# Reordering the first eight loads of a fused attention and gated-MLP kernel: the first Q weights between token tiles 0 and 1, K weights ahead of tile 2

## The chip, the cores and the metric

The kernel runs on one core of a Trainium2 chip. The metric is the device time of one execution in microseconds (us), taken over several executions. A profile gives one of these executions instruction by instruction. Its span is about 1.75 us shorter than the device time of the same execution (268.9 against 270.63 us).

In every text below, tile 0, 1, 2 … are the blocks of 128 tokens of the input, and "Q rows 0-2" are the first three of five 128-row blocks of the Q part of the weight matrix. In profile lines PE is TensorE and PEld its weight loads, DVE is VectorE, ACT is ScalarE, POOL is GpSimd and SP is SyncE; L640 is line 640 of the kernel. XST holds the token tiles as loaded, XNS normalised, XNT also transposed; PS is PSUM, the memory that PE writes its results to.

## The reference, cut to what matters

```python
xn = _layernorm(x)                       # 2048 tokens x 640
qkv = xn @ wqkv                          # 640 -> 3 x 640: Q, K, V
# 32 heads of 20, each token attends to itself and 7 earlier ones, two apart; softmax; weighted V; @ wo
g, u = xn @ w_gate, xn @ w_up            # 640 -> 1536 each
return x + attention(...) @ wo + (g * u) @ w_down
```

Only the head matters here: a token tile is loaded, normalised, transposed, and multiplied by Q, K and V weights.

## The kernel before

The Python program holds a small list scheduler. Each piece of work is a task with a priority, and the scheduler, using its own model of durations and landings, fixes at build time the order of instructions on each engine. So a change in the order of loads changes the *modelled* landings, and through them the order of instructions on all engines.

The loads at the head, all issued by SyncE on one queue:

```python
def x_load(t, eng="sp"):                       # one token tile, 160 KB
    dma(XST[:, xslot(t), :], xhbm[t * TS:(t + 1) * TS, :], ...)

def wqkv_load(g, lo=0, hi=NCH):                # g: 0 Q, 1 K, 2 V; rows lo..hi of five, 160 KB each
    dst = WQKV[:, WPOS[g], lo:hi, :]
    dma(dst, wqkv_src[:, lo:hi, g * D:(g + 1) * D], ...)
# ... cut ...
x_load(0)
# a small touch load on ACT's queue
x_load(1)
wqkv_load(0, 0, 3)
wqkv_load(0, 3, NCH)
x_load(2)
wqkv_load(1, 0, 3)
wqkv_load(1, 3, NCH)
x_load(3)
K.t["act"] = 2.1
warm(18)                                       # 18 filler matmuls on zeros
```

What happens to a tile (cut to the engines and their order):

```python
def front(t):
    # DVE: bn_stats of two halves (L538), bn_aggr (L541); ACT: sqrt (L544); DVE: reciprocal (L549)
    # DVE: apply -> XNS (L556); PE: five transposes into PSUM (L585); tile 0: three filler matmuls (L624)
    # copy out of PSUM -> XNT: tile 0 DVE three blocks (L595) and ACT two (L597); others DVE (L604)
    for i in range(2):
        # ... cut ...
        yield Task("dve", lambda: stats(i), r=[x], prio=-1 if t == 1 and i == 0 else p)
```

The first half of tile 1's statistics has the priority -1: once tile 0's square root is scheduled, it goes ahead of all that is left of tile 0 on DVE. Then PE multiplies (L640): for tile 0, twenty 128-column matmuls with Q, twenty with K; the same for tile 1; ten 256-column matmuls for both tiles together; then tiles 2, 3 and so on, and after them V with 512 columns.

## Time and profile before

| | |
|---|---|
| time, median of 3 (lowest to highest) | 270.04 us (269.69 to 270.15) |
| span of the profiled execution | 268.9 us |
| PE busy | 262.7 us, 98% |
| first projection matmul starts | 7.30 us |
| loss between tile 1's transposes and its first matmul | 0.75 us |

Two lines of the page of the kernel before: busy time of the engines, and the chain of waits that ended last, by engine.

```profile
PE 262.7 (98%) x1765; PEld 152.8 (57%) x1783; DVE 222.9 (83%) x282; ACT 105.4 (39%) x188; POOL 130.3 (48%) x81
...
PE 94%; DMA 2%; DVE 2%; issue 1%; SPq 0%; DVEq 0%
```

PE is busy 98% of the span and makes 94% of the chain. What can be won or lost is therefore the time before PE's unbroken run begins. The timeline of the kernel before, at its head; the columns are start, duration, engine, line, operation, output and inputs, form, count, and in brackets the idle time of that engine just before and what ended it.

```profile
3.22 0.89 DVE L538 BATCH_NORM_STATS2 STATS<-XST 128x6 f32<-128x320 bf16 x2 [1.98 <-DMA XST<-in_A_x_dram]
...
5.42 0.71 PE L585 MATMUL PS<-IDENT,XNS 128*128 128x128 bf16 x5
...
5.96 0.36 DVE L595 COPY XNT<-PS 128x384 bf16<-128x384 bf16 x1 [0.20 <-PE PS L585]
...
7.30 1.48 PE L640 MATMUL PS<-XNT,WQKV 128*128 128x128 bf16 x20 [0.53 <-DMA WQKV<-in_A_wqkv_dram]
...
8.61 0.44 PE L585 MATMUL PS<-IDENT,XNS 128*128 128x128 bf16 x5
...
9.09 0.49 DVE L604 COPY XNT<-PS 128x640 bf16<-128x640 bf16 x1
...
9.64 1.98 PE L640 MATMUL PS<-XNT,WQKV 128*128 128x128 bf16 x32 [0.59 <-DVE XNT L604]
```

Read PE's lines. Its first projection matmul at 7.30 waits for weights although tile 0's copy ended at 6.32 (5.96 + 0.36). Tile 1's transposes come at 8.61; their copy on DVE runs from 9.09 to 9.58, and PE sits idle 0.59 us until it restarts at 9.64. The last transpose began at 8.84 and would have freed PE 0.06 us later, so 0.75 us are lost from start to start. From 9.64 the matmuls follow each other without a gap. The chain of waits of the same kernel in its first 30 us (start, length, what) says the same:

```profile
1.73 5.44 DMA WQKV<-in_A_wqkv_dram
...
9.09 0.50 DVE XNT L604
```

The first line is the load of Q rows 0-2: issued at 1.73, landed at 7.17.

### The profile page before, as it was taken

What the parts mean: (1) busy time and instruction counts of PE and PEld (TensorE: products, weight loads), DVE (VectorE), ACT (ScalarE), POOL (GpSimd) and SP (SyncE); (2) the same over time, 40 slices, a digit from 0 to 9 for tenths busy, and PEclk for the clock granted to TensorE, in tenths of its full rate; (3) what the DMA queues carried; (4) which work ended last, traced back from release to release, by engine and by line L of the source; (5) the groups of instructions that cost most, each with busy time, mean ns of one, the idle gap of its engine ahead of it and who ended that gap; (6) DMA issues with size and microseconds to landing.
All of it is one profiled execution on the core that took longest, in us unless ns stands there. A gap on an engine that the chain in (4) does not pass through costs nothing.

```text
span 268.9 us, 4464 instructions
## 1 busy us (share of the span) xinstructions
PE 262.7 (98%) x1765; PEld 152.8 (57%) x1783; DVE 222.9 (83%) x282; ACT 105.4 (39%) x188; POOL 130.3 (48%) x81
## 2 busy tenths in 40 slices
PE   7899999999999999999999999999999999999996
PEld 5796975444444444444444445765457654676775
DVE  4678899999999997379999899999999989992212
ACT  3369998556723232245344353024430342201000
POOL 1000000000004439900199999999999879985000
PEclk9999999999999999999999999999999999999999
DMA  6954479621414998087025953465534561022201
GB/s 206 367 188 74 98 105 339 247 97 56 142 39 113 234 244 177 0 268 151 2 52 140 240 118 79 132 176 138 152 79 130 148 195 42 27 73 61 87 28 49
DMA packets 40261, 35.58 MB, mean 132 GB/s; under 512 B 15408, under 2 KB 38448, under 8 KB 40240
## 3 DMA queue, kind: packets, MB, share of 16 engines
q1 hardware_dynamic: 39424, 33.15, 45.4%
q0 software_dynamic: 576, 2.10, 3.9%
q8 instruction: 14, 0.23, 0.4%
q10 hardware_dynamic: 240, 0.05, 0.1%
q14 instruction: 7, 0.06, 0.1%
HBM read 25.07 MB, written 5.26 MB: 113 GB/s over the span
## 4 chain that ended last, share of the span: by engine, by line
PE 94%; DMA 2%; DVE 2%; issue 1%; SPq 0%; DVEq 0%
PE PS L1149 36%; PE PS L1231 28%; PE PS L640 24%; PE PS L903 3%; DMA WQKV<-in_A_wqkv_dram 2%; PE PS L1098 2%; DVE HT L1158 1%; PE PS L585 0%; DVE RS L952 0%; DVE LOG L956 0%; SPq L463 0%; DVE XNT L604 0%; DVE SM L932 0%; DVE FOUT L1244 0%; DVEq L325 0%
## 5 line engine op out<-in xcount | busy, mean ns | idle before, releaser
L1056 POOL TENSOR_TENSOR SV<-PV 128x1024 bf16<-128x1024 f32 x40 | 93.5, 2366 | 24.7 <-DVE LOG L956 18.7
L1051 DVE TENSOR_TENSOR PV<-VX,PS 128x1024 f32<-128x1024 bf16 (+1 forms) x56 | 91.8, 1670 | 0.3 <-POOL SV L1056 0.3
L640 PE MATMUL PS<-XNT,WQKV 128*128 128x512 bf16 (+2 forms) x474 | 66.4, 299 | 1.6 <-DVE XNT L604 0.6
L1149 PE MATMUL PS<-XNT,WU 128*128 128x512 bf16 x239 | 59.6, 380 | 0.2
L1149 PE MATMUL PS<-XNT,WG 128*128 128x512 bf16 x229 | 57.3, 380 | 0.7 <-issue 0.3
L640 PEld LDWEIGHTS PS<-XNT,WQKV 128*128 128x128 bf16 x480 | 43.6, 113 | 23.8 <-DVE SD L549 1.0
L1149 PEld LDWEIGHTS PS<-XNT,WU 128*128 128x128 bf16 x240 | 23.3, 98 | 28.7 <-ACT XNT L645 0.8
L1149 PEld LDWEIGHTS PS<-XNT,WG 128*128 128x128 bf16 x240 | 23.2, 98 | 28.6 <-issue 0.8
L792 DVE TENSOR_TENSOR PRD<-QT,KT 128x2048 bf16<-128x2048 bf16 x32 | 36.8, 1217 | 0.0
L1244 DVE TENSOR_TENSOR FOUT<-PS,XR 128x320 bf16<-128x320 f32 (+1 forms) x33 | 15.7, 479 | 22.2 <-PE PS L1231 22.0
L1231 PE MATMUL PS<-WD,HT 128*128 128x320 bf16 x192 | 28.7, 300 | 0.0
L645 ACT ACTIVATE HT<-PS 128x512 bf16<-128x512 f32 x24 | 14.3, 596 | 34.0 <-PE PS L1149 34.0
L1231 PE MATMUL PS<-WO,OT 128*128 128x320 bf16 (+1 forms) x165 | 27.0, 296 | 0.0
L863 POOL TENSOR_TENSOR PRF<-PRF,PRF 128x1024 f32<-128x1024 f32 x4 | 9.4, 2352 | 33.1 <-DVE PRF L837 33.0
L1107 ACT ACTIVATE OT<-PS 128x512 bf16<-128x512 f32 x20 | 10.5, 600 | 34.4 <-PE PS L1098 34.4
L922 POOL MEMSET LOG<- 32x6 bf16 (+6 forms) x7 | 0.4, 95 | 48.4 <-ACT LOG L914 48.4
L1158 DVE TENSOR_TENSOR HT<-HT,PS 128x512 bf16<-128x512 bf16 x24 | 16.3, 680 | 8.7 <-PE PS L1149 7.0
L1231 PEld LDWEIGHTS PS<-WD,HT 128*128 128x128 bf16 x192 | 18.8, 98 | 7.6
L1231 PEld LDWEIGHTS PS<-WO,OT 128*128 128x128 bf16 x165 | 15.7, 98 | 6.6 <-issue 0.8
L837 DVE TENSOR_TENSOR PRF<-PS,KT 128x1024 f32<-128x1024 f32 x16 | 19.0, 1216 | 0.4 <-DMA PRF<-PRF 0.4
L538 DVE BATCH_NORM_STATS2 STATS<-XST 128x6 f32<-128x320 bf16 x32 | 14.7, 471 | 3.0 <-DMA XST<-in_A_x_dram 3.0
L1231 PE MATMUL PS<-WD,XNT 128*128 128x320 bf16 (+1 forms) x108 | 14.6, 285 | 0.0
(58 smaller groups left out, 216.1 us busy)
## 6 DMA issues: line engine op xcount, KB each, us to landing
VX<-v_scratch SPq DMA_DIRECT2D x80, 130.0 KB, 2.9
XST<-in_A_x_dram SPq DMA_DIRECT2D x16, 160.0 KB, 6.2
v_scratch<-VST SPq DMA_DIRECT2D x4, 640.0 KB, 4.3
XR<-in_A_x_dram SPq DMA_DIRECT2D x16, 160.0 KB, 2.9
out_dram<-FOUT SPq DMA_DIRECT2D x15, 160.0 KB, 1.8
PRF<-PRF POOLq DMA_DIRECT2D x4, 512.0 KB, 8.6
WG<-in_B_w_gate_dram SPq DMA_DIRECT2D x1, 1920.0 KB, 8.6
WU<-in_B_w_up_dram SPq DMA_DIRECT2D x1, 1920.0 KB, 12.1
```

What stands on the lines that cost most here:

```text
L538: op("dve", lambda e: e.bn_stats(o, a), r=[a], w=[("st", t, i)], name=f"bn{t}_{i}", occ=0.49)
L640: op("pe", (lambda o, l, x, c, first: lambda e: e.matmul(o, l, x, start=first, stop=(c == NCH - 1)))(o, l, x, c, first), r=[l, x], w=[o], ...
L645: X = op("act", (lambda o, i: lambda e: e.activation(o, i, ACT.Copy))(o, i), r=[i], w=[o], name=name, occ=0.12 + n * 0.9e-3)
L792: op("dve", lambda e: e.tensor_tensor(s[:], qb, kv, ALU.mult), r=[q, rk], w=[s[:]], name=f"prod{j}_{r}_{c}", occ=1.15, lock=True)
L837: X = op("dve", lambda e: e.tensor_tensor(o[:], qb, kv, ALU.mult), r=[q, rk], w=[o[:]], name=f"prow{j}_{r}_{c}_{q0}", occ=1.17)
L1051: op("dve", lambda e: e.tensor_tensor(p, vw, a, ALU.mult), r=[vv] + rk, w=[p], name=f"pv{u}_{x}_{r0}", occ=0.09 + 1.1 * nr)
L1056: X = op("pool", lambda e: e.tensor_tensor(o, p[:, :, 0, :], p[:, :, 1, :], ALU.add), r=[p[:]] + tokens(), w=[o], name=f"pva{u}_{x}", occ= ...
L1107: X = op("act", (lambda o, b: lambda e: e.activation(o, PS[:, b, :], ACT.Copy))(o, b), r=[PS[:, b, :]], w=[o], name=f"oev{u}", occ=0.58)
L1149: op("pe", (lambda l, x, c: lambda e: e.matmul(PS[:, b, :], l, x, start=(c == 0), stop=(c == NCH - 1)))(l, x, c), r=[l, x], w=[PS[:, b, :] ...
L1158: X = op("dve", lambda e: e.tensor_tensor(h, h, PS[:, hold[1], :], ALU.mult), r=[h, PS[:, hold[1], :]], w=[h], name=f"h{m}_{j}", occ=0.65)
L1231: op("pe", (lambda l, x, i: lambda e: e.matmul(dst, l, x, start=(i == 0), stop=(i == n - 1)))(l, x, i), r=[l, x], w=[PS[:, b, :]], name=f" ...
L1244: X = op("dve", lambda e: e.tensor_tensor(o, PS[:, b, 0:wid], xr, ALU.add), r=[PS[:, b, :], xr], w=[o], name=f"fin{t}_{nb}", occ=0.15 + wi ...
```

## The change

Its intent: the first Q weights should be there when tile 0 has been normalised, and K's weights should not stand behind tile 2, which PE needs later than K.

```diff
     x_load(0)
     # touch load on ACT's queue
+    wqkv_load(0, 0, 3)
     x_load(1)
-    wqkv_load(0, 0, 3)
     wqkv_load(0, 3, NCH)
-    x_load(2)
     wqkv_load(1, 0, 3)
     wqkv_load(1, 3, NCH)
+    x_load(2)
     x_load(3)
```

The scheduler answers with another order on every compute engine. Up to the first tiles, PE now does: tile 0 with Q, tile 1's transposes, tile 0 with K and tile 1 with both (60 matmuls), ten 256-column ones, and only then tile 2's transposes. Before, tile 2's transposes stood between matmuls of tiles 0 and 1.

## The prediction

> **What bounds it now.** TensorE. The page gives PE busy 262.7 of 268.9 us (98%), granted clock 1.0, and the chain of waits is 94% PE. The windows table shows PE busy for 29.8 of 30 us (17.9 to 47.8), and so on to the end; real idle time lies only in the first 10 us. So the change can act only through the time at which PE's uninterrupted run starts. After that everything downstream, DVE included, shifts along.
>
> **Head of before (timeline, order of time).** First token tile landed 3.20, second 3.61. The first projection matmul waited 0.53 us for Q rows 0-2 and started at 7.30; its operand, tile 0's transposed copy, was done on DVE at 6.32. Q rows 3-4 landed 8.03 (a further 0.19 us stall). Tile 1's transposes ended 8.9; PE then lost 0.75 us (0.59 idle) waiting for their copy to 9.64. From there it runs; V projections start at 20.86.
>
> **What landings hide.** Each load's semaphore gets 16 increments, one per DMA engine. For Q rows 0-2, 15 came by 5.80 and the sixteenth at 7.17; one packet begun at 3.56 took 2.05 us. Every later load carries that straggler (K rows 0-2 at 9.80, tile 2 at 8.46). This agrees with the Trainium skill, "DMA: Bandwidth & Descriptors", section "Queues, rings and completion order": each engine consumes its own ring in order.
>
> **What the change moves.** No work is added; bytes and matmul counts stay. A 160 KB tile takes 0.44 us of queue time (spacing of landings). With the same straggler I estimate: Q rows 0-2 6.7, tile 1 7.2 (was 3.61), Q rows 3-4 8.0 (unchanged), K 9.35 and 10.3 (0.45 earlier), tile 2 10.7 (was 8.46), tile 3 11.15 (unchanged).
>
> **The catch is DVE's static order** (instruction order of the changed kernel): the first half of tile 1's statistics now stands, with its wait for tile 1's landing, *ahead* of tile 0's copy out of PSUM. In before tile 1 was long there; now a late tile 1 blocks tile 0. Estimate with the straggler:
> - tile 1 lands 7.2; statistics 0.45, copy 0.36: first projection matmul 8.1 (+0.8), its 20 matmuls x 56 ns to 9.2;
> - rest of statistics 0.5, aggregate 0.2, square root 0.3, reciprocal 0.16, apply 0.45: tile 1's transposes at 9.8, 0.6 us of PE idle;
> - tile 0's K matmuls now fill the wait for tile 1's copy (saves 0.75);
> - tile 2's transposes are now followed at once by a matmul that needs their copy: a new 0.75 us stall near 14.6;
> - V projections near 21.9, about 1.0 later than before.
>
> If no packet straggles in typical runs of either kernel, tile 1 lands near 5.8 and the same sums give about +0.45; if it only vanishes in the new one, -0.5.
>
> **Later.** The order of gate/up and down matmuls differs, with the same counts. In before each group of weighted-value matmuls began 0.8 to 2.2 us after its POOL producer ended, so I expect no new stall above 0.3 us, but a changed order could cost or win some tenths.
>
> **Prediction:** 270.9 us, range 269.7 to 272.0. Faster by over 2%: 0.005; within 2%: 0.975; slower by over 2%: 0.02.
>
> **Right or wrong shown by:** first projection matmul start (about 8.1 against 7.30) and its releaser, DVE's copy, which itself follows statistics waiting for the second tile; PE idle before tile 1's transposes; a stall after tile 2's transposes; V start near 21.9; from there to the end the same 248 us.
>
> **Would make it wrong:** the straggler falling elsewhere or not at all, so that tile 1 lands near 5.4 and Q starts before 7; tile 1's landing being too early to block; the later reordering opening or closing a stall of 1 us.

## The result, and the profile after

| | before | after |
|---|---|---|
| median of 6 runs (lowest to highest) | 270.12 us (269.69 to 270.40) | 270.25 us (269.96 to 270.36) |
| ratio, 95% interval | | 1.0003 (0.999 to 1.0016) |
| span of the profiled execution | 268.9 us | 268.5 us |

A ratio is the mean time of one kernel's runs over that of the other's in the same rounds, so it is not quite the ratio of the medians. The time lies in the predicted range, and the forecast of "within 2%" holds; but the point forecast (+0.9 us) is too high, and the first profile even shows a span shorter by 0.4 us. Both had to be explained. The same two lines of the page of the changed kernel:

```profile
PE 264.0 (98%) x1783; PEld 153.0 (57%) x1783; DVE 223.0 (83%) x282; ACT 105.2 (39%) x188; POOL 130.4 (49%) x81
...
PE 96%; DMA 2%; SPq 1%; DVE 0%; issue 0%
```

Its timeline, the lines that answer to those above:

```profile
5.52 0.49 DVE L538 BATCH_NORM_STATS2 STATS<-XST 128x6 f32<-128x320 bf16 x1 [0.22 <-DMA XST<-in_A_x_dram]
...
5.93 0.34 DVE L595 COPY XNT<-PS 128x384 bf16<-128x384 bf16 x1
...
6.50 1.46 PE L640 MATMUL PS<-XNT,WQKV 128*128 128x128 bf16 x20
...
7.98 0.45 PE L585 MATMUL PS<-IDENT,XNS 128*128 128x128 bf16 x5
...
8.47 0.49 DVE L604 COPY XNT<-PS 128x640 bf16<-128x640 bf16 x1 [0.55 <-PE PS L585]
...
8.63 4.64 PE L640 MATMUL PS<-XNT,WQKV 128*128 128x128 bf16 x70 [0.20 <-DMA WQKV<-in_A_wqkv_dram]
...
13.10 0.44 PE L585 MATMUL PS<-IDENT,XNS 128*128 128x128 bf16 x5
...
13.58 0.49 DVE L604 COPY XNT<-PS 128x640 bf16<-128x640 bf16 x1 [0.35 <-PE PS L585]
...
14.13 1.31 PE L640 MATMUL PS<-XNT,WQKV 128*128 128x128 bf16 x20 [0.59 <-DVE XNT L604]
```

Four things are to be seen. DVE did wait for tile 1 before tile 0's copy, as predicted, but only 0.22 us, since tile 1 landed at 5.49 and not at 7.2. The first projection matmul started at 6.50, not at 8.1, and it had no named wait: PE was still doing its three filler matmuls. After tile 1's transposes PE now waits for K's weights (0.20 us, until 8.63). And the new stall behind tile 2's transposes is there: 0.59 us idle, until 14.13. In the chain of waits the releaser has changed to the load of K rows 0-2 (issued 2.73, landed 8.58), and tile 2's copy has taken the place of tile 1's:

```profile
2.73 5.85 DMA WQKV<-in_A_wqkv_dram
...
13.58 0.50 DVE XNT L604
```

The landings come from the sixteen semaphore increments of each load, read from the trace:

| load | before: 15th, 16th increment | after: 15th, 16th |
|---|---|---|
| tile 0 | 3.12, 3.20 | 3.10, 3.13 |
| Q rows 0-2 | 5.80, **7.17** | 4.95, 5.06 |
| tile 1 | 3.60, 3.61 | 5.39, 5.49 |
| Q rows 3-4 | 6.67, 8.03 | 6.55, 6.82 |
| K rows 0-2 | 9.08, 9.80 | 8.32, 8.58 |
| tile 2 | 7.07, 8.46 | 9.67, 9.90 |

The Trainium skill, "DMA: Bandwidth & Descriptors", section "Why a DMA increments its semaphore by 16 and not by 1", says that only the full 16 means that all data has landed. In the trace PE's first matmul was let go accordingly, at the sixteenth (7.17), 1.37 us behind the fifteenth; that some data was really missing until then no run here tests. In the execution of the changed kernel no early load had such a lag.

The rest of the program does not take part. In all traces with complete records, V's first matmul is followed by the last PE instruction 245.65 us later: in both kernels and in both parts of the change. From V's start to the end of the span it is 248.24 us (one variant below, 248.66, aside). The first profile of before lacks 18 PE records, the first V matmul among them; its V start is 268.89 - 248.24 = 20.65 us (the prediction's 20.86 is the first V matmul that this trace still has). The changed kernel's is 20.28. So the difference of two spans is the difference of two heads, and 21 us of a 270 us kernel are all there is to study.

### The profile page after: what moved, and what is told of

Read it like the earlier page. It is cut to its first block, busy times and chain, and to the rows that moved or that the text cites. A ratio compares the mean times of both kernels' runs of the same rounds, so it can differ in the third digit from the quotient of the medians.

```text
span 268.5 us, 4477 instructions
## 1 busy us (share of the span) xinstructions
PE 264.0 (98%) x1783; PEld 153.0 (57%) x1783; DVE 223.0 (83%) x282; ACT 105.2 (39%) x188; POOL 130.4 (49%) x81
## 4 chain that ended last, share of the span: by engine, by line
PE 96%; DMA 2%; SPq 1%; DVE 0%; issue 0%
PE PS L1149 39%; PE PS L1231 28%; PE PS L640 24%; PE PS L903 3%; DMA WQKV<-in_A_wqkv_dram 2%; PE PS L1098 2%; SPq L463 1%; PE PS L585 0%; DVE XNT L604 0%; DVE FOUT L1244 0%
## 5 line engine op out<-in xcount | busy, mean ns | idle before, releaser
L1149 PE MATMUL PS<-XNT,WG 128*128 128x512 bf16 x240 | 59.7, 379 | 0.0
L837 DVE TENSOR_TENSOR PRF<-PS,KT 128x1024 f32<-128x1024 f32 x16 | 19.1, 1218 | 0.5 <-DMA PRF<-PRF 0.5
L538 DVE BATCH_NORM_STATS2 STATS<-XST 128x6 f32<-128x320 bf16 x32 | 14.6, 471 | 3.1 <-DMA XST<-in_A_x_dram 3.1
```

The source lines that it names most:

```text
L538: op("dve", lambda e: e.bn_stats(o, a), r=[a], w=[("st", t, i)], name=f"bn{t}_{i}", occ=0.49)
L837: X = op("dve", lambda e: e.tensor_tensor(o[:], qb, kv, ALU.mult), r=[q, rk], w=[o[:]], name=f"prow{j}_{r}_{c}_{q0}", occ=1.17)
L1149: op("pe", (lambda l, x, c: lambda e: e.matmul(PS[:, b, :], l, x, start=(c == 0), stop=(c == NCH - 1)))(l, x, c), r=[l, x], w=[PS[:, b, :] ...
```

## Experiments

Twelve runs were made, in three calls of four (three of them repeat the two kernels unchanged); each call was on one chip, with 11 runs of the kernel before beside them. All twelve gave correct results. "V" is the start of the V projections; where 18 records were missing, it is worked out as span - 248.24. To move instructions without changing anything else, a helper lifts already scheduled operations, with their dependencies, to another place in the emission order:

```python
def place(names, before=None, after=None):     # K.ops: all operations in order; waits are derived later
    ops = K.ops
    first = {}
    for X in ops:
        first.setdefault(X.name, X)
    moved = [first[n] for n in names]
    for X in moved:
        ops.remove(X)
    at = ops.index(first[before or after]) + (before is None)
    ops[at:at] = moved
```

My theory at the start (1): the late sixteenth increment was an accident of the profiled execution. Rival (2): the lag belongs to the old queue order and the change removes it.

| run | ratio to before (95%) | first projection matmul | PE restarts after tile 1's transposes | V |
|---|---|---|---|---|
| before, first profile | – | 7.30 | 9.64 | 20.65 |
| before_again | 1.0006 (0.9993–1.0019) | 6.51 | 8.73 | 19.73 |
| after, first profile | 1.0003 (0.999–1.0016) | 6.50 | 8.63 | 20.28 |
| after_again | 1.0021 (1.0009–1.0033) | 6.37 | 9.01 | 20.66 |
| after_third | 1.0024 (1.0011–1.0038) | 6.50 | 9.03 | 20.68 |
| queue_only | 1.0109 (1.0084–1.0133) | 8.51 | 11.97 | 23.41 |
| compute_only | 1.0043 (1.0031–1.0055) | 7.03 | 9.50 | 21.15 |
| x1_late | 1.0046 (1.0031–1.0061) | 7.26 | 9.21 | 20.92 |
| x1_late_free | 1.0032 (1.0019–1.0044) | 6.54 | 8.84 | 20.56 |
| after_free | 1.0011 (0.9999–1.0023) | 6.21 | 8.55 | 20.28 |
| after_fill | 1.0005 (0.9991–1.0019) | 6.90 | 8.84 | 20.39 |
| after_free_fill | 1.0007 (0.9995–1.0019) | 6.36 | 8.68 | 20.12 |
| before_tuned | 0.9992 (0.9977–1.0006) | 7.22 | – | 20.15 |
| tuned_split | 1.0020 (1.0009–1.0032) | 6.13 | – | 20.28 |

(In before_tuned and tuned_split the transposes stand in the middle of tile 0's matmuls, so there is no such restart.)

### Both kernels again: before_again, after_again

No edit. Expected of before_again:

> The kernel before, unchanged, for a second profile. Theory 1 (the late sixteenth increment of the first profile is an accident of that execution): Q rows 0-2 land within 0.4 us of their fifteenth increment, near 5.5 to 5.9 us, the first projection matmul starts at 6.5 to 6.7, V projections at 19.9 to 20.4, and the span is 0.3 to 0.8 us shorter than the 268.9 of the first profile. Theory 2 (this queue order always has the straggler): last increment over 1 us late again, V at about 20.9, span 268.9. Timed ratio to before: 1.000 in both.

Expected of after_again:

> The changed kernel, unchanged, for a second profile. Theory 1: the head can now show the straggler or not; if it does not, V starts at 20.3 and span 268.3 to 268.6 as in the first; if it does fall on tile 1, V at 21 to 22 as predicted. Theory 2 (this queue order never has it): V at 20.3 again. Timed ratio 1.000 to 1.002.

Measured: before_again 269.90 us median, after_again 270.62 us. The second execution of before, PE's timeline:

```profile
6.51 1.36 PE L640 MATMUL PS<-XNT,WQKV 128*128 128x128 bf16 x20
...
8.73 1.98 PE L640 MATMUL PS<-XNT,WQKV 128*128 128x128 bf16 x32 [0.59 <-DVE XNT L604]
```

Q rows 0-2 landed at 6.25 (fifteenth increment 6.01): no large lag, but later than the 5.5 to 5.9 expected. PE started at 6.51 and restarted at 8.73. V came at 19.73, 0.9 us earlier than in the first profile and a little earlier than expected (19.9 to 20.4). So the head of the unchanged kernel moves by 0.9 us between two executions, more than the change is worth. The second execution of the changed kernel:

```profile
6.37 1.29 PE L640 MATMUL PS<-XNT,WQKV 128*128 128x128 bf16 x20
8.00 0.45 PE L585 MATMUL PS<-IDENT,XNS 128*128 128x128 bf16 x5 [0.34 <-DVE XNS L556]
9.01 4.64 PE L640 MATMUL PS<-XNT,WQKV 128*128 128x128 bf16 x70 [0.56 <-DMA WQKV<-in_A_wqkv_dram]
...
14.51 1.31 PE L640 MATMUL PS<-XNT,WQKV 128*128 128x128 bf16 x20 [0.58 <-DVE XNT L604]
```

Here the lag fell on K rows 0-2 (fifteenth increment 7.88, sixteenth 8.97), and PE idled 0.56 us for it. V at 20.66 is neither of the cases that I had named (20.3 without a lag, 21 to 22 with one on tile 1), and it is against rival 2's "20.3 again". The lag is not a fixture of the old queue order alone: the new one can have it too, on another load. Theory 1 is not the whole truth either: see the end of this section.

### The change in halves: queue_only, compute_only

queue_only is the kernel before with the eight loads emitted in the new order and every compute engine in its old order; compute_only is the opposite. The edit of queue_only, in front of the emission (compute_only puts the old order into the changed kernel):

```diff
+    want = ('xld0', 'ld_wqkv0_0', 'xld1', 'ld_wqkv0_3', 'ld_wqkv1_0', 'ld_wqkv1_3', 'xld2', 'xld3')
+    at = [i for i, X in enumerate(K.ops) if X.name in want]
+    made = {K.ops[i].name: K.ops[i] for i in at}
+    for i, n in zip(at, want):
+        K.ops[i] = made[n]
     K.emit(stores)
```

> The new order of the eight loads on the queue, with the instruction order of the kernel before on every compute engine. If the compute order that comes with the change is what hides the later tiles (my theory): DVE's tile 1 statistics block tile 0's normalisation, tile 2's block tile 1's copy; first projection matmul at about 7.9, stall before tile 1's projections until about 11.0, V at about 22.2, time 1.5 to 2.3 us above before (ratio 1.006 to 1.008). Rival (the order of loads hardly matters as TensorE is busy 98% of the span): ratio 1.000 to 1.002.

Measured: 272.83 us, ratio 1.0109, about 3 us slower. First DVE, then PE of queue_only:

```profile
6.28 0.49 DVE L538 BATCH_NORM_STATS2 STATS<-XST 128x6 f32<-128x320 bf16 x1 [2.13 <-DMA XST<-in_A_x_dram]
...
10.41 0.49 DVE L538 BATCH_NORM_STATS2 STATS<-XST 128x6 f32<-128x320 bf16 x1 [1.02 <-DMA XST<-in_A_x_dram]
```

```profile
7.37 0.71 PE L585 MATMUL PS<-IDENT,XNS 128*128 128x128 bf16 x5 [2.08 <-DVE XNS L556]
...
8.51 2.34 PE L640 MATMUL PS<-XNT,WQKV 128*128 128x128 bf16 x20
...
11.97 2.42 PE L640 MATMUL PS<-XNT,WQKV 128*128 128x128 bf16 x32 [0.59 <-DVE XNT L604]
```

DVE's old order puts tile 1's first statistics even ahead of tile 0's reciprocal and apply. Tile 1 landed at 6.25, so DVE stood idle 2.13 us, tile 0's transposes slipped to 7.37 and the first projection matmul to 8.51. Then DVE waited 1.02 us for tile 2, whose statistics stand ahead of tile 1's copy. The mechanism is as expected, the size larger (V at 23.41 instead of 22.2). The rival, "the order of loads hardly matters", falls.

Part of that size is something else. In this execution PE issued one 128-column matmul every 107 ns until 12.9 us; the other kernels' PE was at 56 ns by 7.3 us. So DVE, done with tile 2's first statistics at 10.90, still had to wait for tile 1's transposes:

```profile
11.43 0.49 DVE L604 COPY XNT<-PS 128x640 bf16<-128x640 bf16 x1 [0.52 <-PE PS L585]
```

From the restart to V it then took 11.44 us (23.41 - 11.97), against 11.00 in the kernel before. My estimate from these two figures is that the slow PE cost about 1.0 us (0.5 + 0.4) of the 3.7 us by which V is later than in before_again. The two slowest of the six timed runs (273.50 and 273.93 us) are also those with a granted clock under 1.0 (0.994 and 0.987). So not all of the 1.1% is waiting for loads. Whether PE's 2.08 us of idle time before 7.37 made it late is not tested.

> The new instruction order on the compute engines with the old order of the loads. My theory: first projection matmul at about 6.4 (no blocking, tile 1 landed at 3.6), then K rows 0-2 land about 0.45 us later than in the changed kernel and tile 0's K matmuls wait for them until 9.0 or so; the stall of about 0.6 us after tile 2's transposes stays; V at about 20.7, time 0.3 to 0.6 us above before (ratio 1.001 to 1.003). Rival (the loss in the changed kernel comes from the blocking by tile 1's late landing): V at 19.9 or earlier and ratio below 0.999.

Measured: 271.11 us, ratio 1.0043. PE of compute_only:

```profile
7.03 1.41 PE L640 MATMUL PS<-XNT,WQKV 128*128 128x128 bf16 x20 [0.88 <-DMA WQKV<-in_A_wqkv_dram]
...
9.50 4.64 PE L640 MATMUL PS<-XNT,WQKV 128*128 128x128 bf16 x70 [0.78 <-DMA WQKV<-in_A_wqkv_dram]
...
15.00 1.31 PE L640 MATMUL PS<-XNT,WQKV 128*128 128x128 bf16 x20 [0.59 <-DVE XNT L604]
```

Tile 1 is early and blocks nothing, as expected, but Q rows 0-2 landed at 6.89, so PE started at 7.03 and not at 6.4; then it waits 0.78 us for K rows 0-2 (landed 9.45), and the 0.59 us behind tile 2's transposes are there as well. The rival, that blocking by tile 1 is the loss in the changed kernel, predicted a gain here, and there is none. This run alone does not refute it, because K also landed 0.9 us later than in the changed kernel (9.45 against 8.58) and set the restart. But in all three profiles of the changed kernel, too, the restart waits for K's landing (0.20, 0.56 and 0.62 us idle) and not for the blocked copy.

The two halves alone cost 1.1% and 0.4%; together they cost 0.0 to 0.2%. The new instruction order is made for the new landings. With both, about half or more of what either half loses is gone.

### Is the predicted blocking real, and does it bite: x1_late, x1_late_free, after_free

x1_late makes tile 1 land later in the changed kernel; x1_late_free also takes tile 1's first statistics from in front of tile 0's copy; after_free does only the latter.

```diff
+    place(["xld1"], after="ld_wqkv0_3")        # x1_late and x1_late_free
+    place(["bn1_0"], after="xntcp0_0")         # x1_late_free and after_free
     K.emit(stores)
```

> The changed kernel with the second tile put one place later on the queue, behind Q rows 3-4 (tile 1 lands near 6.35 instead of 5.49 us); all compute orders as in the changed kernel. If the blocking of tile 0's copy by tile 1's statistics is real (the prediction's mechanism), the copy starts at about 6.85 and the first projection matmul at about 7.3 (6.4 to 6.5 in the changed kernel), a delay of nearly the whole 0.86 us; V at 20.8 to 21.1, ratio 1.003 to 1.004. If blocking does not matter, the first projection matmul stays at 6.5 and V at 20.3 to 20.7.

Measured: 270.88 us, ratio 1.0046. DVE and PE of x1_late:

```profile
6.46 0.49 DVE L538 BATCH_NORM_STATS2 STATS<-XST 128x6 f32<-128x320 bf16 x1 [1.10 <-DMA XST<-in_A_x_dram]
6.87 0.34 DVE L595 COPY XNT<-PS 128x384 bf16<-128x384 bf16 x1
```

```profile
7.26 1.31 PE L640 MATMUL PS<-XNT,WQKV 128*128 128x128 bf16 x20 [1.07 <-DVE XNT L595]
```

Tile 1 landed at 6.43. DVE waited 1.10 us, copied at 6.87, and PE started at 7.26 after 1.07 us idle. This is the predicted chain, step by step. The ratio is a little above the 1.003 to 1.004 expected.

> As x1_late, but tile 1's first statistics stand behind tile 0's copy on DVE. Copy at 5.93 and first projection matmul at 6.5 again, whatever tile 1 does. Blocking theory: V about 0.3 us earlier than in x1_late (not 0.8, because tile 1's own chain of statistics, square root and apply then sets the transposes at 8.5), ratio 1.002 to 1.003. If the lateness of tile 1 itself, not the blocking, is the whole cost, V equals that of x1_late.

Measured: 270.62 us, ratio 1.0032. PE of x1_late_free:

```profile
6.54 1.28 PE L640 MATMUL PS<-XNT,WQKV 128*128 128x128 bf16 x20
8.54 0.45 PE L585 MATMUL PS<-IDENT,XNS 128*128 128x128 bf16 x5 [0.72 <-DVE XNS L556]
8.84 4.72 PE L640 MATMUL PS<-XNT,WQKV 128*128 128x128 bf16 x70
```

With the statistics out of the way PE started at 6.54, 0.72 us earlier than in x1_late. But it then waited 0.72 us for tile 1's own normalisation before the transposes, and V came only 0.36 us earlier (20.56 against 20.92, expected 0.3). The blocking is real; about half of what it delays would be lost to the late tile anyway. This rests on the traces: the intervals of the two ratios (1.0031 to 1.0061 and 1.0019 to 1.0044) overlap.

> The changed kernel with tile 1's first statistics behind tile 0's copy on DVE (the blocking undone), queue order unchanged. With tile 1 landing at 5.5 the blocking costs nothing: DVE finishes the statistics at 6.0 while TensorE still works through tile 0's transposes and three filler matmuls until 6.5; ratio within 0.001 of after_third. If the blocking as predicted were the main cost, the ratio would fall by 0.002 or more.

Measured: 270.25 us, ratio 1.0011, beside 1.0024 for after_third on the same chip. The ratios differ by 0.0013, a little more than the 0.001 I had allowed, and the intervals overlap. PE of after_free:

```profile
6.21 1.31 PE L640 MATMUL PS<-XNT,WQKV 128*128 128x128 bf16 x20
8.26 0.45 PE L585 MATMUL PS<-IDENT,XNS 128*128 128x128 bf16 x5 [0.73 <-DVE XNS L556]
8.55 4.72 PE L640 MATMUL PS<-XNT,WQKV 128*128 128x128 bf16 x70
```

Its first matmul began at 6.21 because in this execution PE reached full rate before the transposes (see the last section). Then it waited until 8.26 for tile 1's normalisation. From there the work is the same: tile 0's K matmuls began at 8.55 because K rows 0-2 had landed at 8.30; in after_third they landed at 8.98. So the earlier V of this execution (20.28 against 20.68) is K's landing to the extent that the trace can tell. Whether the blocking costs anything at the usual landing of 5.5 us is not decided by these times; a gain of 0.2% and more is not supported.

after_third, the companion:

> The changed kernel once more, as the companion of the next two on the same chip and for a third sample of its landings. If it is a little slower than before as a rule, ratio 1.000 to 1.0025 and span 248.24 us behind the start of V; V at 20.3 without a straggler on tile 1 or K, up to 21.3 with one.

Measured: 270.78 us, ratio 1.0024; tile 1 landed at 5.47, K rows 0-2 at 8.98, PE idled 0.62 us for them.

### Is tile 2's exposed copy a loss: after_fill, after_free_fill

```diff
+    place(["sd2", "rstd2", "lnap2"], after="bn3_0")           # only shifts ACT against one evacuation
+    place(["pev1_0"], after="sd2")
+    place([f"tr2_{c}" for c in range(5)], before="p0_0_4_0")  # ahead of the ten 256-column matmuls
     K.emit(stores)
```

> The changed kernel with tile 2's transposes moved ahead of ten 256-column matmuls that need only tiles 0 and 1 (1.07 us of work to cover tile 2's copy), and tile 2's square root ahead of one evacuation on ACT. If the exposed copy of tile 2 is a real loss: the 0.59 us idle at about 14.1 goes, V 0.5 to 0.65 us earlier than in the changed kernel under the same landings (19.7 to 20.1), ratio 0.9985 to 1.0005. If tile 2's late landing (9.9 to 10.3) is the limit instead, the idle only moves ahead of the transposes and V stays at 20.3 to 20.7.

Measured: 270.04 us, ratio 1.0005 (another chip than after_third, so only a hint). PE of after_fill:

```profile
6.90 1.47 PE L640 MATMUL PS<-XNT,WQKV 128*128 128x128 bf16 x20 [0.26 <-DVE XNT L595]
...
12.48 0.45 PE L585 MATMUL PS<-IDENT,XNS 128*128 128x128 bf16 x5
12.77 2.37 PE L640 MATMUL PS<-XNT,WQKV 128*128 128x256 bf16 x30
15.37 0.45 PE L585 MATMUL PS<-IDENT,XNS 128*128 128x128 bf16 x5 [0.22 <-DVE XNS L556]
```

The 0.59 us behind tile 2's transposes are gone. This execution also shows the blocking at its natural size: tile 1 landed at 6.07, and PE started only at 6.90, after 0.26 us idle behind DVE's copy. What the edit won is seen by measuring from the restart to V, where both kernels have the same work left: 20.39 - 8.84 = 11.55 us, against 20.28 - 8.63 = 11.65 in the changed kernel. That is 0.1 us, not 0.6; PE also stood still for 0.1 us just after the restart here (0.162 instead of 0.056 us between the matmuls at 8.90 and 9.06), and without that it would be 0.2. Tile 2 landed at 9.82 and its apply ended at 12.43 (the 12.48 of the transposes is that); the last of the 60 matmuls before them began at 12.28, so at 0.056 us a matmul the transposes now wait about 0.15 us, hidden in the timeline because a matmul's recorded duration overlaps the next one; and tile 3's transposes idle 0.22 us. My expectation failed: the idle time in good part only moves. Its rival blamed tile 2's late landing, but the trace names another cause, tile 2's and tile 3's square roots on ACT:

```profile
11.78 0.16 DVE L549 RECIPROCAL SD<-SD 128x1 f32<-128x1 f32 x1 [0.44 <-ACT SD L544]
...
14.66 0.16 DVE L549 RECIPROCAL SD<-SD 128x1 f32<-128x1 f32 x1 [1.20 <-ACT SD L544]
```

Tile 2's aggregate was done at 10.98, but on ACT an evacuation (the copy of finished Q products out of PSUM, 10.97 to 11.57) came first, and the square root began at 11.46. The 0.44 us that DVE waited for it are more than the 0.15 us that the transposes waited. Tile 3's square root (14.34) likewise came behind two evacuations, although its aggregate was done at 13.07. No run moved these square roots further ahead.

> Both edits on the changed kernel: no blocking, and tile 2's copy covered by the ten 256-column matmuls. Expected: the idle of 0.59 us after tile 2's transposes gone, V at 19.7 to 19.9 without a straggler and 0.5 to 0.6 us before that of after_third under equal landings; ratio to before 0.999 to 1.000. If it stays at after_third's ratio, the exposed copy was not the loss.

Measured: 270.15 us, ratio 1.0007 beside 1.0024 for after_third; V at 20.12, 11.44 us behind the restart. Against the 11.65 us of the changed kernel that is 0.2 us. The hoped-for 19.7 to 19.9 was missed; tile 1 had landed at 6.01. Here tile 2 (landed at 10.00) had its square root without delay (aggregate done at 11.16, square root at 11.20), so its landing did set its transposes (12.22, 0.16 us late by the spacing of the matmuls); tile 3's again waited for ACT (1.20 us). It is not faster than before.

### Can the head of before be shortened: before_tuned, tuned_split

```diff
+    place(["bnag1", "sd1"], after="bn1_1")                    # on the kernel before
+    place(["rstd1", "lnap1"], after="xntcp0_0")
+    place([f"tr1_{c}" for c in range(5)], before="p0_0_0_3")  # after 12 of tile 0's 20 Q matmuls
+    place(["bn2_0"], after="xntcp1")
     K.emit(stores)
```

> The kernel before, its queue order kept, with tile 1's normalisation hurried: its aggregate and square root ahead of tile 0's copies, its transposes after 12 instead of 20 of tile 0's Q matmuls, tile 2's statistics behind tile 1's copy. If what bounds the head of before is tile 1's exposed copy (0.59 us idle in both profiles), V comes to 19.1 to 19.3 with no straggler (19.73 before) and the ratio is 0.997 to 0.9985. If K's landing (9.0) bounds it instead, the gain is under 0.2 us and the ratio 0.999 to 1.001.

Measured: 269.61 us against 269.78, ratio 0.9992 with an interval across 1. PE of before_tuned:

```profile
7.22 0.84 PE L640 MATMUL PS<-XNT,WQKV 128*128 128x128 bf16 x12 [1.07 <-DMA WQKV<-in_A_wqkv_dram]
7.89 0.44 PE L585 MATMUL PS<-IDENT,XNS 128*128 128x128 bf16 x5
```

Q rows 0-2 landed at 7.08 in this execution. From the first projection matmul to V it took 20.15 - 7.22 = 12.93 us, against 13.35 in the first profile of before (20.65 - 7.30) and 13.22 in the second: 0.3 to 0.4 us saved. The expected 19.1 to 19.3 for V was meant for a kernel without a late Q load and was missed. The edit does what it should in the trace; in the times its gain is not proved. The lowest of all its runs, 269.13 us, is the lowest time of any run.

tuned_split also cuts the load of Q rows 0-2 into three:

```diff
-    wqkv_load(0, 0, 3)
+    wqkv_load(0, 0, 1)
+    wqkv_load(0, 1, 2)
+    wqkv_load(0, 2, 3)
```

> before_tuned (queue order of before, tile 1 hurried) with the load of Q rows 0-2 cut into three of one row each, so that the first four matmuls wait for a third of the bytes. If the straggler on Q rows 0-2 is what before_tuned lost its gain to, the first projection matmul starts at 6.3 to 6.6 even when row 2 lands at 7.1, and the ratio is 0.997 to 0.9985 (0.9992 measured for before_tuned). If two more issues of about 0.5 us on the queue delay K and the later tiles, K rows 0-2 land 0.5 us or more later and the ratio is 1.000 or above.

Measured: 270.65 us, ratio 1.0020: a loss. PE of tuned_split:

```profile
6.13 0.87 PE L640 MATMUL PS<-XNT,WQKV 128*128 128x128 bf16 x12
...
7.75 1.73 PE L640 MATMUL PS<-XNT,WQKV 128*128 128x128 bf16 x28 [0.38 <-DMA WQKV<-in_A_wqkv_dram]
10.13 0.86 PE L640 MATMUL PS<-XNT,WQKV 128*128 128x128 bf16 x12 [0.65 <-DMA WQKV<-in_A_wqkv_dram]
```

The first matmul did come at 6.13, but Q rows 3-4 landed at 7.61 and K rows 0-2 at 10.08, and PE waited 0.38 and 0.65 us for them. The issue of K rows 0-2 had slipped from 3.25 to 4.15 us, but their packets also shared the queue with a late engine (fifteenth increment 9.28), so one execution does not separate the two. A further 0.4 us went at the very end, in SyncE's closing drain (0.5 us instead of 0.16), for which I have no reason.

### What stays open

Q rows 0-2, loaded whole, landed at 6.25 to 7.17 us in the four traces with the old order of the queue, and at 5.04 to 5.83 in the nine with the new one. One place on the queue explains 0.44 us of this (the spacing of two tile landings); the gap between the middle values, 6.99 and 5.16, is 1.8 us. In the first profile one packet, begun at 3.56, took 2.05 us. So the lag is more common on this load in the old order than my theory 1 had it, but not bound to it, and why is not known. The gap between the last two increments does not show all of it: in compute_only it was 0.01 us on this load, but these two came 0.8 us behind the fourteenth. No run here tried other loads in that place.

## Why the prediction was right or wrong, point by point

- **What bounds the kernel**: right. Everything behind V's start is constant, 248.24 us of span in both kernels; the prediction said "the same 248 us". The feared "later reordering" of gate/up and down matmuls cost nothing.
- **The direction and the class**: right, by a little. Three same-round ratios of the changed kernel are 1.0003, 1.0021 and 1.0024; two of the three intervals lie above 1. Over all runs on all chips the medians are 269.91 us (45 runs) and 270.36 us (17 runs): about +0.45 us, 0.2%; by the ratios, it ran from +0.1 to +0.65 us. The prediction said +0.9.
- **The step that failed**: "tile 1 lands 7.2 … first projection matmul 8.1 (+0.8)". Tile 1 landed at 5.47 to 5.49 in three profiles of the changed kernel, Q started at 6.37 to 6.50, and the DVE block cost 0.17 to 0.22 us of DVE's time. I took the lag of one execution's load as a property of the queue at that moment and handed it to whatever load came there. Eight more traces of kernels that put Q second on the queue, besides the first one of the changed kernel, show a lag of 0.04 to 0.8 us on Q rows 0-2 between fifteenth and sixteenth increment, none of 1.37.
- **The alternative sum in the prediction**, "if no packet straggles in typical runs of either kernel … about +0.45", gave the size that was measured. That the figures agree is partly luck: this sum had tile 1 at 5.8 (5.47 to 5.49 measured) and no wait for K (0.20 to 0.62 us measured), and the two pairs of profiles, taken in the order they were made, differ at V by -0.37 and +0.93 us. Still, it should have been the main line, or the two should have been weighed by a second profile.
- **The blocking by DVE's order**: the mechanism was right (x1_late, x1_late_free, and after_fill by chance). In the three profiles of the changed kernel it cost PE nothing that the trace names; in after_fill, with tile 1 at 6.07, it cost 0.26 us. What it costs in the times is not decided (after_free).
- **"Tile 0's K matmuls now fill the wait for tile 1's copy (saves 0.75)"**: half right. The wait for the copy is gone, but PE waits for K's landing instead: 0.20, 0.56 and 0.62 us idle. Starting Q earlier had made K the next limit, which the prediction, with Q at 8.1, could not see.
- **"A new 0.75 us stall near 14.6"**: right. It is 0.75 us beyond the usual spacing from the last transpose to the next matmul, ending at 14.13 to 14.53 in the three profiles of the changed kernel, and it is as long in compute_only, x1_late, x1_late_free and after_free, which keep that order.

The gain and the loss can now be put in one sum, since both kernels have the same work left when PE restarts after tile 1's transposes. In before V comes 11.00 us after the restart (9.64 to 20.65; 8.73 to 19.73). In the changed kernel it is 11.65 us in all three traces (8.63 to 20.28, 9.01 to 20.66, 9.03 to 20.68), and so it is in compute_only (9.50 to 21.15); in x1_late, x1_late_free and after_free it is 11.71 to 11.73. So the new order of work loses 0.65 us, and the new order of loads must win it back through an earlier restart. It does when the old order's Q load is late (8.63 against 9.64: the first pair of profiles, span 0.4 us shorter) and does not when Q lands by 6.3 (9.01 against 8.73: the second pair, 0.9 us longer). In that second pair K's lag took part as well: with the 8.63 of the other profile, V would still be 0.55 us later (20.28 against 19.73). That is why the profiles of the first pair contradict the times: the profiled execution of before, 270.63 us, was slower than every one of its six timed runs in that comparison.

## What to carry to other kernels

Before explaining a load's landing, take a second profile of the unchanged kernel: here two executions of one program differed by 0.9 us at the head, twice what the change was worth. When loads are reordered under a static instruction order, look for an instruction that now waits for a later load and stands in front of work that was ready; and after pulling one load forward, ask which load is the next to be waited for. A stall that can be covered on paper may only move to the next wait (here a late landing, or a square root that stood behind other work on ACT), so compare the time from a common restart to a common end, not the idle time alone.

## What the Trainium skill lacked or had wrong

- "DMA: Bandwidth & Descriptors" (sections "Why a DMA increments its semaphore by 16 and not by 1" and "Queues, rings and completion order") gives the rule that sixteen increments make a landing and that each engine consumes its ring in order. The runs are in line with both, though the trace does not tell which engine an increment came from (the lag of Q rows 0-2 came back on Q rows 3-4, fifteenth 6.67 and sixteenth 8.03, and on tile 2, 7.07 and 8.46). The page has no figure for how far the last engine of an ordinary load from HBM trails the others, nor that this varies from one execution to the next: on the early weight and tile loads it was 0.0 to 1.4 us here, with one packet of 2.05 us.
- The same page, section "Latency and other measured facts", knows two DMA engines that are usually slower and gives a guess that is specific to loads issued from GpSimd. The late loads here were issued by SyncE. Which engine was late the trace doesn't tell, so the two can't be joined.
- "TensorE: Matmul & The Clock Gate", section "What's actually happening", calls the array's warm-up run-variable. That agrees: tile 0's transposes were issued every 107 ns in nine of the fourteen executions in the table and every 56 ns in the other five; with the faster ones the three filler matmuls behind them ended sooner, which took part in the first projection matmul's range from 6.13 to 6.54 us where no load held it up. A warning that belongs to the profile's table and not to the page: it shows a granted clock of 1.00 from 0 to 7.3 us in the kernel before, but the trace has no clock record before 6.77 us there, so that 1.00 is no measurement. The first record comes where the matmuls speed up: at 6.87 us in the first profile of the changed kernel (spacing 107 ns until 6.8, 56 ns from 6.9), at 12.96 in queue_only (107 ns until 12.9).
- No page says how a static instruction order on a compute engine interacts with the order of loads. The numbers are in queue_only: the same loads that cost 0.0 to 0.2% with their own instruction order cost 1.1% with the old one (part of it PE's slower rate in that run).
